# Attention and gated MLP on one core: scores from the ninth pair on as three rounded products in place of one f32 product

## The chip, the cores and the metric

The kernel runs as one program on one core of a Trainium2 chip. The metric is device time in microseconds, from the program's start to its end, the median of several runs. The profile shows one further execution, instruction by instruction.

## The reference

Eight batches of eight heads go through causal attention with decay; the eight heads of a batch are then laid side by side and go through a gated MLP with a product over the sequence.

```python
batch, n_heads, seq, head_dim = (8, 8, 576, 64)

scores = scale * np.matmul(q, k.transpose(0, 1, 3, 2))
log_f = np.log(np.clip(f, 0.0001, 1.0))
cum = np.cumsum(log_f, axis=-1)
decay = cum[:, :, :, None] - cum[:, :, None, :]
scores = np.where(causal, -1000000000.0, scores + decay)
attn = np.exp(scores - max); attn = attn / (sum + 1e-09)
x = np.matmul(attn, v)            # heads side by side: 576 x 512 per batch

h = np.maximum(x @ w_in, 0.0)     # w_in 512 x 1024
u, v = (h[..., :512], h[..., 512:])
v_n = (v - mu) / np.sqrt(var + 1e-06)
v_s = np.einsum('ts,bsd->btd', w_spatial, v_n) + b_spatial[None, :, None]
return (u * v_s) @ w_out
```

All inputs and outputs are float32.

## The kernel before

The 64 heads are worked on as 32 pairs, P = 0 to 31; four pairs make a batch. A pair's q and k lie transposed in one tile `qk_t` (128 partitions x 1216 columns, L239): head 0 on partitions 0 to 63, head 1 on 64 to 127, 640 columns of q and 576 of k. In the last 128 columns of q the 64 tail queries of each head stand in a block of their own, with zeros beside them, so that one product over all 128 partitions gives the tail of both heads.

The scores of a pair are made in three parts. `score_piece` (L316) makes the causal blocks i = 0 to 3, of 128 queries and 128 (i + 1) keys, for each head from its own 64 partitions. The *first piece* is i = 2, 1, 0 (products of 384, 256 and 128 columns for each head), the *second piece* is i = 3 (512 columns). `scores_tail` (L362) makes the *tail* in two products of 288 columns (L370, traced under the helper's line L233). Each product is one f32 matmul, which the trace shows as two matmul instructions. `in_one_piece` (L217) keeps the products of a piece together and lets the first one wait for the readers that free its PSUM banks; banks 0 and 1 also hold the attention product, and DVE's subtraction into `xl` (L513) frees them.

Behind the scores, DVE's `lowest` (L306) adds the decay tile `dk` or `dt` and takes the row minimum, ACT makes the exponentials (L337, the tail's L375), DVE the reciprocals (L352, L353), and POOL multiplies by them (`share`, L314). From P = 8 on (`moved`, L393) DVE transposes the weights in 32 x 32 blocks into `mid` (L456, the tail also L381), and SP's queue moves them by 16 transfers into `e` (L463), from where PE makes the attention product (L488, L493). Its result is split into a rounded high part `xh` (fp32r, ACT, L510) and a rest `xl` (DVE, L513). The MLP, called expert work here, uses such pairs everywhere: each of its products is three fp32r matmuls (L233), high by high, high by rest, rest by high, one matmul instruction each.

`attention` (L714) works on pair P and makes the scores of P + 1: it prepares P + 1 (`prep`, L237: transfers of `qk_t`, `dk`, `dt`), masks the decay tiles on POOL (`mask`, L275, lines L280, L282, L286, called *selects* below), sends the weights of P to `e`, makes the scores of P + 1 with their tail, and then the attention product of P. The driver at the end (L874) interleaves the units of `attention` with those of `moe` (L744) by their progress. A scheduler then fixes the order on each engine, so the order of the rows is part of what a change changes. Within each engine instructions run in order.

Buffers that the change touches: `qk_t` has two buffers under the tag "qk"; the small tiles `nm` and `sm` six each; the output tile `o` (L847) two; `load_rest` (L176) brings the remaining weights through the tags "gt0", "gt1" and "o", with 1, 1 and 2 buffers; a tile of zeros `zm` (L63), read only by warming matmuls in the first stage, lives for the whole program.

Of the kernel before, what the change touches and what calls it, by code (L numbers as in the profile page):

```python
# [23 lines left out]
TL = 512  # L24
# [14 lines left out]
def attn_gmlp_kernel(ctx: ExitStack, tc: tile.TileContext, qk, v, f, w_in, w_sp, b_sp, w_out, out):  # L39
# [21 lines left out]
    make_identity(nc, ident)  # L61

    zm = cst.tile([128, 512], BF16, name="zm")  # L63
    G.memset(zm, 0.0)

# [110 lines left out]
    def load_rest(n, w_v, dh, dl, mark=None):  # L176

        raw = mo.tile([128, 2, 128, 2], U32, name="w64", tag=("gt0", "gt1", "o")[n % 3], bufs=(1, 1, 2)[n % 3])
        w = mo.tile([128, 2, 128], U32, name="w32", tag="GH", bufs=3)
        t = mo.tile([128, 2, 128], U32, name="wa", tag="GH", bufs=3)  # L180
        r, c = slice(2 * (n % 2), 2 * (n % 2) + 2), slice(128 * (n // 2), 128 * (n // 2) + 128)
        load64(w_v[:, r, c, :], dh[:, r, c], dl[:, r, c], raw, w[:], t[:], mark)
# [54 lines left out]
    def prep(P):  # L237

        qk_t = wk.tile([128, QK], F32, name="qk_t", tag="qk", bufs=2)  # L239
        SY.dma_start(out=qk_t, in_=qk[P])  # L240
        yield
# [11 lines left out]
        for h in range(2):  # L253
            SY.dma_start(out=dt[64 * h:64 * h + 64, :], in_=row_of(P, h, 640, S, 64))
        yield

    def columns(rt):
# [51 lines left out]
    def share(P, t, r):  # L309
# [3 lines left out]
        else:  # L313
            G.tensor_scalar(out=t, in0=t, scalar1=r, scalar2=1.0, op0=ALU.mult, op1=ALU.mult)  # L314

    def score_piece(P, qk_t, piece):  # L316

# [4 lines left out]

        def product(i, h):
            ps, c, _ = at[i, h]
            p, n = slice(64 * h, 64 * h + 64), 128 * (i + 1)
            return lambda: T.matmul(ps[:, c:c + n], qk_t[p, n - 128:n], qk_t[p, 640:640 + n], start=True, stop=True)  # L326

        in_one_piece([product(i, h) for i in reversed(piece) for h in range(2)])
        return at
# [9 lines left out]
    def scores(P):  # L339

        qk_t, dk, _ = tab[P]
        tt, _ = turn(P)
        nm = [wk.tile([128, 4], F32, name="nm", tag="nm", bufs=6) for h in range(2)]
        sm = [wk.tile([128, 4], F32, name="sm", tag="sm", bufs=6) for h in range(2)]
        for piece in ((0, 1, 2), (3,)):
# [16 lines left out]
    def scores_tail(P):  # L362
        qk_t, _, dt = tab.pop(P)
        _, tl = turn(P)
        nm = wk.tile([128, 4], F32, name="nm", tag="nm", bufs=6)
        sm = wk.tile([128, 4], F32, name="sm", tag="sm", bufs=6)
        for j in range(2):
            k0 = 288 * j
            sc = bank(2 + j)
            mm(sc[:, 0:288], qk_t[:, TL:640], qk_t[:, 640 + k0:928 + k0], True, True)  # L370
            freed[2 + j] = lowest(tl[:, k0:k0 + 288], sc[:, 0:288], dt[:, k0:k0 + 288], nm[:, j:j + 1])
            yield 485
# [13 lines left out]
    def keep_warm(n):  # L386
        for _ in range(n):
            mm(warm[0], zm[:, 0:128], zm[:, 0:512], True, True)

# [136 lines left out]
    def first(ws):  # L526
# [23 lines left out]
        def period(P):  # L550
# [7 lines left out]
            sb = wk.tile([128, 2, 1], F32, name="sb", tag="sb", bufs=2)  # L558
            nt = wk.tile([128, 4], F32, name="nm", tag="nm", bufs=6)
            st = wk.tile([128, 4], F32, name="sm", tag="sm", bufs=6)  # L560

# [89 lines left out]
            late.append((X, st))  # L651

        for c in range(NJ):
            blocks[c] = load_first(ws, c)
# [11 lines left out]
        rt = next(rows)  # L666
        warm.append(bank(5, False))
        keep_warm(16)
# [75 lines left out]
    def moe(b):  # L744
# [89 lines left out]
        if b % 2 == 1:  # L834
            yield from w_out_tile(b, *[[g[:, j, :] for j in range(NJ)] for g in gt[0]],
                                  [(b - 1, TL, 0, 64), (b, TL, 64, 64)])

    def w_out_tile(b, ghi, glo, dst):
        ps = acc(b)
        n = 0  # L840
        for j in range(NJ):
# [3 lines left out]
            yield 648  # L845
        tag, bufs = ("vx", 2) if b == B - 1 and nps[0] % 3 else ("o", 2)
        o = mo.tile([128, DM], F32, name="o", tag=tag, bufs=bufs)  # L847
# [78 lines left out]
```

## Time and profile before

| what | value |
|---|---|
| median of 3 runs | 746.35 us (745.24 to 753.86) |
| the profiled execution | 752.48 us, of which the span from first to last instruction is 750.3 |
| PE, matmuls | 700.4 us busy (93%), 4709 instructions |
| DVE / POOL / ACT | 480.3 / 380.1 / 369.2 us busy |
| mean granted clock of PE | 0.979 of full speed |
| L326, the two pieces, PE | 512 instructions |
| L233 `sc<-qk_t`, the tail, PE | 128 instructions |

The profile gives for every instruction its start and duration; times are in microseconds from the start of the span. Matmuls are pipelined, so the step from one matmul's start to the next one's says what a matmul costs, not its duration. PEld is the weight load of PE, SPq the DMA queue of SP. In a waits view, "A <- B" means that A sat idle until B ended.

### The profile page before, as it was taken

The numbers are of one execution on the slowest core, as the hardware profiler recorded it, in microseconds if no ns is written. First come the engines' busy times: TensorE is split into PE (matmuls) and PEld (weight loads), VectorE is DVE, ScalarE is ACT, GpSimd is POOL, SyncE is SP. The second block draws the span as 40 slices with busy tenths as digits, with TensorE's granted clock in tenths as the row PEclk, the third lists the DMA queues.
The fourth block names the chain that finished last, engine by engine and source line by source line (L and its number), as shares of the span: only waits on it lengthen the run. The fifth ranks groups of instructions, "written<-read, shape, count | busy, mean of one in ns | idle before, by whom it ended". The sixth has DMA issues, their size and how long they took to land.

```text
span 750.3 us, 14594 instructions
## 1 busy us (share of the span) xinstructions
PE 700.4 (93%) x4709; PEld 554.1 (74%) x4709; DVE 480.3 (64%) x1597; ACT 369.2 (49%) x1028; POOL 380.1 (51%) x703
## 2 busy tenths in 40 slices
PE   7878979789989898999999999999999999999997
PEld 3545757558778586797778777788779787899886
DVE  6787787855676575667666766767666766821332
ACT  6866586663544344645444444544454435521231
POOL 3887555584554453544475454635464455611241
PEclk9999999999999899999999999999999999999999
DMA  7855344246657777557874687657965686330001
GB/s 234 240 151 144 108 145 133 78 127 184 191 160 188 194 188 206 155 147 204 213 204 136 179 220 226 178 114 203 227 172 151 176 226 178 84 88 29 29 1 70
DMA packets 52749, 117.82 MB, mean 157 GB/s; under 512 B 10305, under 2 KB 14401, under 8 KB 52674
## 3 DMA queue, kind: packets, MB, share of 16 engines
q1 hardware_dynamic: 48082, 108.64, 53.7%
q10 hardware_dynamic: 4592, 8.26, 3.2%
q8 instruction: 37, 0.61, 0.4%
q14 instruction: 38, 0.31, 0.2%
HBM read 67.78 MB, written 9.75 MB: 103 GB/s over the span
## 4 chain that ended last, share of the span: by engine, by line
PE 52%; DVE 8%; POOL 8%; ACT 6%; issue 5%; DMA 2%; SPq 2%; ACTq 0%; POOLq 0%; DVEq 0%
PE ps L233 34%; PE sc L326 6%; PE sc L488 5%; POOL tt L314 4%; PE sc L233 3%; ACT tt L337 3%; DMA e<-mid 2%; PE tp L233 2%; DVE mid L456 2%; SPq L463 1%; PE sc L493 1%; DVE tt L306 1%; POOL vnl L782 1%; DVE st L774 1%; ACT o L851 1%
## 5 line engine op out<-in xcount | busy, mean ns | idle before, releaser
L337 ACT ACTIVATE tt<-tt,nm 128x384 f32<-128x384 f32 (+2 forms) x240 | 132.7, 554 | 69.0 <-DVE nm L306 66.4
L314 POOL TENSOR_SCALAR tt<-tt,sm 128x128 f32<-128x128 f32 x208 | 110.0, 549 | 49.3 <-DVE sm L353 47.0
L456 DVE STREAM_TRANSPOSE mid<-tt 128x128 f32<-128x128 f32 x192 | 90.7, 494 | 30.7 <-POOL tt L314 26.1
L827 POOL TENSOR_TENSOR gl<-u,gh 128x256 fp32r<-128x256 f32 (+1 forms) x64 | 51.4, 805 | 100.7 <-ACT gh L826 99.6
L326 PE MATMUL sc<-qk_t 64*128 64x128 f32 (+3 forms) x512 | 90.3, 473 | 9.2 <-DVE nm L306 4.8
L233 PE MATMUL ps<-xh,winh 128*128 128x256 f32 (+1 forms) x232 | 71.8, 312 | 4.2 <-DVE vx L772 2.8
L233 PE MATMUL ps<-sph,vnh 128*128 128x256 f32 (+1 forms) x240 | 74.1, 309 | 0.7 <-ACT o L851 0.7
L326 PEld LDWEIGHTS sc<-qk_t 64*128 64x128 f32 x512 | 46.1, 194 | 38.6 <-issue 9.5
L306 DVE CUSTOM_DVE_ANT_1 tt<-sc,dk 128x256 f32<-128x256 f32 (+1 forms) x120 | 64.8, 550 | 13.5 <-PE sc L326 9.8
L233 PE MATMUL ps<-xh,winl 128*128 128x256 f32 (+1 forms) x232 | 70.2, 303 | 2.9 <-POOL winl L144 2.8
L233 PE MATMUL ps<-spl,vnh 128*128 128x256 f32 (+1 forms) x240 | 70.8, 295 | 0.0
L233 PE MATMUL ps<-sph,vnl 128*128 128x256 f32 (+1 forms) x240 | 70.5, 294 | 0.0
L488 PE MATMUL sc<-e,vraw 128*64 128x256 f32 (+1 forms) x576 | 65.6, 348 | 4.8 <-DVE nm L306 2.3
L233 PE MATMUL ps<-xl,winh 128*128 128x256 f32 (+1 forms) x232 | 69.9, 302 | 0.0
L826 ACT CAST gh<-u 128x256 fp32r<-128x256 f32 (+1 forms) x64 | 27.3, 431 | 68.2 <-DVE u L823 36.2
L233 PE MATMUL ps<-winh,xh 128*128 128x512 f32 x148 | 59.9, 405 | 0.4 <-ACT o L851 0.4
L782 POOL TENSOR_TENSOR vnl<-vx,vnh 128x512 fp32r<-128x512 f32 x32 | 41.0, 1287 | 35.7 <-ACT vnh L780 35.7
L306 DVE CUSTOM_DVE_ANT_0 tt<-sc,dk 128x128 f32<-128x128 f32 (+1 forms) x120 | 48.7, 419 | 14.9 <-PE sc L326 13.6
L233 PE MATMUL ps<-winl,xh 128*128 128x512 f32 x148 | 57.8, 390 | 0.0
L823 DVE TENSOR_TENSOR u<-ps,u 128x256 f32<-128x256 f32 (+1 forms) x60 | 26.7, 445 | 47.2 <-PE ps L233 47.2
L510 ACT CAST xh<-sc 128x256 fp32r<-128x256 f32 x64 | 24.9, 399 | 63.4 <-PE sc L488 40.3
L233 PEld LDWEIGHTS ps<-xh,winh 128*128 128x128 f32 x232 | 44.8, 194 | 10.9 <-DVE vx L772 5.4
(223 smaller groups left out, 1771.7 us busy)
## 6 DMA issues: line engine op xcount, KB each, us to landing
e<-mid SPq DMA_DIRECT2D x384, 100.0 KB, 2.2
qk_t<-in_dram SPq DMA_DIRECT2D x32, 608.0 KB, 5.9
dk<-rows_d SPq DMA_DIRECT2D x58, 320.0 KB, 5.3
vraw<-in_dram SPq DMA_DIRECT2D x32, 320.0 KB, 4.0
dt<-rows_d SPq DMA_DIRECT2D x58, 144.0 KB, 6.1
out_dram<-o ACTq DMA_DIRECT2D x28, 256.0 KB, 3.6
w<-in_dram SPq DMA_DIRECT2D x16, 256.0 KB, 3.0
w<-in_dram SPq DMA_DIRECT2D x4, 512.0 KB, 6.5
```

Source lines behind the costliest of these rows:

```text
L233: T.matmul(o, l, r, start=st, stop=sp)
L306: return V.tensor_tensor_reduce(out=out, in0=ps, in1=dec, scale=-0.125, scalar=3.0e38, op0=ALU.add, op1=ALU.min, accum_out=acc_)
L314: G.tensor_scalar(out=t, in0=t, scalar1=r, scalar2=1.0, op0=ALU.mult, op1=ALU.mult)
L326: return lambda: T.matmul(ps[:, c:c + n], qk_t[p, n - 128:n], qk_t[p, 640:640 + n], start=True, stop=True)
L337: last["exp", P, h, i] = A.activation(t, t, AF.Exp, bias=nm, scale=-1.0, accum_out=sm)
L456: V.transpose(out=part(middle(P)[:, 0, at:], [[32, n], [RUN, 4], [1, 32]]), in_=part(t, [[128, n], [32, 4], [1, 32]]))
L488: return lambda: T.matmul(out, vt[:, c, h, :], src, start=c == 0, stop=c == end)
L510: last[P, s0 // 256] = A.copy(xh[:, s0:s0 + n], ps[:, 0:n])
L782: G.tensor_tensor(out=tlo, in0=x, in1=f32(th[:]), op=ALU.subtract)
L823: V.tensor_tensor(out=g, in0=o, in1=g, op=ALU.mult)
L826: A.copy(gh[j][:, 0:nt], g)
L827: G.tensor_tensor(out=gl[j][:, 0:nt], in0=g, in1=f32(gh[j][:, 0:nt]), op=ALU.subtract)
```

## The change

From P = 8 on (`moved(P)`) q and k come into a tile `raw`; ACT casts all 1216 columns to fp32r (`high`), and the rest `low` = raw - high is subtracted by POOL (columns 0 to 639, the q half) and by DVE (576 columns, the k half). Each f32 product of the scores becomes three fp32r products that add up in PSUM: high by high, high by low, low by high. The first product of a pair's first piece waits for both subtractions. `raw` and `low` share the two buffers of `qk_t`; `high` has one buffer. Other buffers change too: `zm` moves into the pool of the first stage, `nm` and `sm` go from six buffers to three and four, the tag "o" from two to one, and outputs take turns between the tags "vx" (two buffers, also used by the normalization) and "o".

```diff
     def prep(P):
 
-        qk_t = wk.tile([128, QK], F32, name="qk_t", tag="qk", bufs=2)
-        SY.dma_start(out=qk_t, in_=qk[P])
+        if moved(P):
+            qk_t = apart(P)
+        else:
+            qk_t = wk.tile([128, QK], F32, name="qk_t", tag="qk", bufs=2)
+            SY.dma_start(out=qk_t, in_=qk[P])
         yield
...
+    apart_by = {}
+
+    def apart(P):
+
+        raw = wk.tile([128, QK], F32, name="raw", tag="qk", bufs=2)
+        low = wk.tile([128, QK], F32R, name="low", tag="qk", bufs=2)
+        high = wk.tile([128, QK], F32R, name="high", tag="high")
+        SY.dma_start(out=raw, in_=qk[P])
+        A.copy(high, raw)
+        apart_by[P] = []
+        for by, c in ((G, slice(0, 640)), (V, slice(640, QK))):
+            apart_by[P].append(by.tensor_tensor(out=low[:, c], in0=raw[:, c], in1=f32(high[:, c]), op=ALU.subtract))
+        return (high, high), (high, low), (low, high)
...
+    def terms_of(P, qk_t):
+        return qk_t if moved(P) else ((qk_t, qk_t),)
+
     def score_piece(P, qk_t, piece):
...
-        def product(i, h):
+        terms = terms_of(P, qk_t)
+
+        def product(i, h, k):
             ps, c, _ = at[i, h]
             p, n = slice(64 * h, 64 * h + 64), 128 * (i + 1)
-            return lambda: T.matmul(ps[:, c:c + n], qk_t[p, n - 128:n], qk_t[p, 640:640 + n], start=True, stop=True)
-
-        in_one_piece([product(i, h) for i in reversed(piece) for h in range(2)])
+            l, r = terms[k]
+            return lambda: T.matmul(ps[:, c:c + n], l[p, n - 128:n], r[p, 640:640 + n], start=k == 0,
+                                    stop=k == len(terms) - 1)
+
+        in_one_piece([product(i, h, k) for i in reversed(piece) for k in range(len(terms)) for h in range(2)],
+                     apart_by.get(P, ()))
         return at
...
-            mm(sc[:, 0:288], qk_t[:, TL:640], qk_t[:, 640 + k0:928 + k0], True, True)
+            terms = terms_of(P, qk_t)
+            for k, (l, r) in enumerate(terms):
+                mm(sc[:, 0:288], l[:, TL:640], r[:, 640 + k0:928 + k0], k == 0, k == len(terms) - 1)
...
-        nm = wk.tile([128, 4], F32, name="nm", tag="nm", bufs=6)
-        sm = wk.tile([128, 4], F32, name="sm", tag="sm", bufs=6)
+        nm = wk.tile([128, 4], F32, name="nm", tag="nm", bufs=3)
+        sm = wk.tile([128, 4], F32, name="sm", tag="sm", bufs=4)
...
-        raw = mo.tile([128, 2, 128, 2], U32, name="w64", tag=("gt0", "gt1", "o")[n % 3], bufs=(1, 1, 2)[n % 3])
+        raw = mo.tile([128, 2, 128, 2], U32, name="w64", tag=("gt0", "gt1", "o")[n % 3])
...
-        tag, bufs = ("vx", 2) if b == B - 1 and nps[0] % 3 else ("o", 2)
+        outs[0] += 1
+        tag, bufs = ("vx", 2) if (nps[0] % 3 if b == B - 1 else outs[0] % 2) else ("o", 1)
```

The scheduler's order moves with it. On PE, ahead of and in the first piece of P = 17, the kernel before has (`woh`, `wol` are MLP weights, `sc` the score banks, `ps` the MLP's):

```order
L233 MATMUL ps<-wol,gh 128x512
L233 MATMUL ps<-woh,gh 128x512
L233 MATMUL ps<-wol,gh 128x512
L326 MATMUL sc<-qk_t 128x384 x2
L326 MATMUL sc<-qk_t 128x256 x2
L326 MATMUL sc<-qk_t 128x128 x2
L233 MATMUL ps<-woh,gl 128x512 x2
L233 MATMUL sc<-qk_t 128x288 x2
L233 MATMUL ps<-sph,vnh 128x320
```

and the changed kernel:

```order
L230 MATMUL ps<-woh,gh 128x512
L230 MATMUL ps<-wol,gh 128x512
L346 MATMUL sc<-high 128x384 x2
L346 MATMUL sc<-low,high 128x384 x2
L346 MATMUL sc<-high,low 128x384 x2
L346 MATMUL sc<-high 128x256 x2
L346 MATMUL sc<-low,high 128x256 x2
L346 MATMUL sc<-high,low 128x256 x2
L346 MATMUL sc<-high 128x128 x2
L346 MATMUL sc<-low,high 128x128 x2
L346 MATMUL sc<-high,low 128x128 x2
L230 MATMUL ps<-woh,gl 128x512 x2
```

The piece stands at the same place, with nine rows of two in place of three (the two of a row are the two heads); the tail's two f32 products, next, become six.

On PE, around the second piece of P = 16, the kernel before has both tail products next to the second piece:

```order
L233 MATMUL ps<-sptb,vb 128x256
L233 MATMUL sc<-qk_t 128x288
L326 MATMUL sc<-qk_t 128x512 x2
L233 MATMUL sc<-qk_t 128x288
L233 MATMUL ps<-sph,vnh 128x256
L233 MATMUL ps<-spl,vnh 128x256
```

In the changed kernel the tail of P = 16 is begun there, and its last two products stand 23 expert matmuls later, directly ahead of the attention product (`e,vraw`):

```order
L230 MATMUL ps<-woh,gl 128x512
L230 MATMUL ps<-woh,gh 128x512
L230 MATMUL ps<-wol,gh 128x512
L230 MATMUL ps<-woh,gl 128x512
L230 MATMUL sc<-low,high 128x288
L230 MATMUL sc<-high,low 128x288
L512 MATMUL sc<-e,vraw 64x4x2x32 x2
L517 MATMUL sc<-e,vraw 64x64 x2
```

So the tail ends later against the second piece than before, by the expert work between.

On POOL, between the shares of P = 16 (`tt_84` and `tt_85` are heads 0 and 1 of the weights, `tl` the tail's) and the first piece of P = 17, the kernel before has:

```order
L280 AFFINE_SELECT dk<-dk 128x2x128
L282 AFFINE_SELECT dk<-dk 128x256
L314 TENSOR_SCALAR tt_85<-tt_85,sm 128x128
L314 TENSOR_SCALAR tt_85<-tt_85,sm 128x256
L314 TENSOR_SCALAR tt_85<-tt_85,sm 128x384
L314 TENSOR_SCALAR tt_85<-tt_85,sm 128x512
L314 TENSOR_SCALAR tl<-tl,sm 128x576
L280 AFFINE_SELECT dk<-dk 128x2x128
L282 AFFINE_SELECT dk<-dk 128x256
L286 AFFINE_SELECT dt<-dt 64x64 x2
L827 TENSOR_TENSOR gl<-u,gh 128x256
```

and the changed kernel, where the two heads are called `tt_82` and `tt_83`:

```order
L294 AFFINE_SELECT dk<-dk 128x2x128
L296 AFFINE_SELECT dk<-dk 128x256
L328 TENSOR_SCALAR tt_83<-tt_83,sm 128x128
L328 TENSOR_SCALAR tt_83<-tt_83,sm 128x256
L328 TENSOR_SCALAR tt_83<-tt_83,sm 128x384
L328 TENSOR_SCALAR tt_83<-tt_83,sm 128x512
L294 AFFINE_SELECT dk<-dk 128x2x128
L296 AFFINE_SELECT dk<-dk 128x256
L268 TENSOR_TENSOR low<-raw,high 128x640
L300 AFFINE_SELECT dt<-dt 64x64 x2
L328 TENSOR_SCALAR tl<-tl,sm 128x576
L853 TENSOR_TENSOR gl<-u,gh 128x256
```

The subtraction into `low` stands behind the selects of `dk` of both heads, and the share of the tail moves from ahead of the second head's selects to behind those of `dt`.

## Rows read from the trace of the kernel before

**Rows 1.** Busy time of the engines from 360 to 420 us.

```profile
core 0: us, PE busy (x) PEld busy (x) DVE busy (x) ACT busy (x) POOL busy (x), PEclk, DMA share, GB/s
360.00:420.00 60.00, 59.11 (x429) 47.45 (x428) 39.20 (x137) 29.55 (x84) 30.50 (x59) 1.00 0.68 180
```

**Rows 2.** PE's waits from 180 to 645 us: total, times, longest (us).

```profile
PE sc L326 <- DVE xl L513: 3.0, 2, 2.4
```

**Rows 3.** Chain of waits around P = 18: start, duration (us), what.

```profile
367.71 1.50 PE sc L326 x12
369.20 1.59 PE ps L233 x6
370.79 0.97 PE sc L233 x4
371.76 1.06 PE sc L326 x4
...
387.08 1.50 PE sc L326 x12
```

**Rows 4.** Chain of waits from P = 28 to P = 29.

```profile
584.31 1.06 PE sc L326 x4
...
586.06 3.70 PE ps L233 x23
...
592.65 3.21 PE ps L233 x13
...
608.90 0.58 PE sc L488 x4
```

**Rows 5.** Timeline of PE: fp32r matmuls of 320 and 256 columns, a load.

```profile
169.39 0.31 PE L233 MATMUL ps<-sph,vnh 128*128 128x320 f32 x1
169.54 0.31 PE L233 MATMUL ps<-spl,vnh 128*128 128x320 f32 x1
...
413.05 0.28 PE L233 MATMUL ps<-sph,vnl 128*128 128x256 f32 x1
413.17 0.28 PE L233 MATMUL ps<-sph,vnh 128*128 128x256 f32 x1
...
413.17 0.19 PEld L233 LDWEIGHTS ps<-spl,vnh 128*128 128x128 f32 x1
```

**Rows 6.** Groups by line and shape: casts and subtractions (busy us, mean ns).

```profile
L143 ACT CAST winh<-w 128x256 fp32r<-128x256 f32 x8 | 3.2, 403 | 2.8 <-POOL w L141 2.8
L159 ACT CAST sph<-wraw 128x576 fp32r<-128x576 f32 x4 | 2.6, 654 | 0.0
...
L144 POOL TENSOR_TENSOR winl<-w,winh 128x256 fp32r<-128x256 f32 x8 | 6.1, 763 | 4.6 <-ACT winh L143 4.6
L160 POOL TENSOR_TENSOR spl<-wraw,sph 128x576 fp32r<-128x576 f32 x4 | 5.7, 1418 | 5.4 <-ACT sph L159 5.4
```

**Rows 7.** Line 786 on DVE: duration in ns, least, median, most.

```profile
L786 DVE TENSOR_TENSOR vnh<-vx,vnh x8: 685/830/1141, 110.7 to 722.8; 64x512 fp32r<-64x512 f32 x8
```

**Rows 8.** Timeline of POOL ahead of P = 17 and P = 29.

```profile
346.40 0.41 POOL L280 TENSOR_SCALAR_AFFINE_SELECT dk<-dk 128x256 f32<-128x256 f32 x1 [1.10 <-DMA dk<-rows_d]
346.76 0.41 POOL L282 TENSOR_SCALAR_AFFINE_SELECT dk<-dk 128x256 f32<-128x256 f32 x1
...
593.18 0.75 POOL L314 TENSOR_SCALAR tl<-tl,sm 128x576 f32<-128x576 f32 x1
...
594.24 0.41 POOL L282 TENSOR_SCALAR_AFFINE_SELECT dk<-dk 128x256 f32<-128x256 f32 x1
```

**Rows 9.** Timeline of PE at the first pieces of P = 17 and P = 29.

```profile
347.33 0.92 PE L326 MATMUL sc<-qk_t 64*128 64x384 f32 x4
...
594.78 0.39 PE L233 MATMUL ps<-woh,gh 128*128 128x512 f32 x1
595.01 0.39 PE L233 MATMUL ps<-wol,gh 128*128 128x512 f32 x1
...
595.79 1.57 PE L326 MATMUL sc<-qk_t 64*128 64x384 f32 x12
```

**Rows 10.** SP's waits from 100 to 200 us: total, times, longest (us).

```profile
SPq L126 <- DVE wa L139: 27.7, 7, 7.2
```

More of the change, by code (lines that the diff above doesn't have):

```diff
@@ L61, in attn_gmlp_kernel @@
     make_identity(nc, ident)
-    zm = cst.tile([128, 512], BF16, name="zm")
-    G.memset(zm, 0.0)
     lnc = cst.tile([128, 3], F32, name="lnc")
@@ L342, in scores @@
         tt, _ = turn(P)
-        nm = [wk.tile([128, 4], F32, name="nm", tag="nm", bufs=6) for h in range(2)]
-        sm = [wk.tile([128, 4], F32, name="sm", tag="sm", bufs=6) for h in range(2)]
+        nm = [wk.tile([128, 4], F32, name="nm", tag="nm", bufs=3) for h in range(2)]
+        sm = [wk.tile([128, 4], F32, name="sm", tag="sm", bufs=4) for h in range(2)]
         for piece in ((0, 1, 2), (3,)):
@@ L387, in keep_warm @@
         for _ in range(n):
-            mm(warm[0], zm[:, 0:128], zm[:, 0:512], True, True)
+            mm(warm[0], warm[1][:, 0:128], warm[1][:, 0:512], True, True)
     nev = [0]
@@ L558, in period @@
             sb = wk.tile([128, 2, 1], F32, name="sb", tag="sb", bufs=2)
-            nt = wk.tile([128, 4], F32, name="nm", tag="nm", bufs=6)
-            st = wk.tile([128, 4], F32, name="sm", tag="sm", bufs=6)
+            nt = wk.tile([128, 4], F32, name="nm", tag="nm", bufs=3)
+            st = wk.tile([128, 4], F32, name="sm", tag="sm", bufs=4)
             def low(i, at):
@@ L651, in period @@
             late.append((X, st))
+        zm = ws.tile([128, 512], BF16, name="zm", bufs=1)
+        G.memset(zm, 0.0)
         for c in range(NJ):
@@ L666, in first @@
         rt = next(rows)
-        warm.append(bank(5, False))
+        warm.extend((bank(5, False), zm))
         keep_warm(16)
@@ L836, in moe @@
                                   [(b - 1, TL, 0, 64), (b, TL, 64, 64)])
+    outs = [0]
     def w_out_tile(b, ghi, glo, dst):
```

## The prediction

> **What bounds the kernel now.** I read the stretches first: from 360 to 420 us the matrix engine PE is busy 59.11 of 60 us, DVE 39.20, POOL 30.50, ACT 29.55 [rows 1]. So where the scores of P = 9 to 31 are made, PE's own time sets the pace. PE's waits agree: the largest between 180 and 645 us is 3.0 us in all, for DVE's `xl` [rows 2]. The chain through P = 18 shows what a pair's scores cost there: 1.50 us for the first piece (12 f32 matmul instructions, two to a product), 0.97 for the tail (4), 1.06 for the second piece (4); the next first piece starts at 387.08, 15 us after this second piece [rows 3]. Last I looked at a pair with less room ahead of it, P = 29: the second piece of P = 28 at 584.31, the tail's rest, 23 expert matmuls, the attention product, 13 expert matmuls [rows 4], and the first piece of P = 29 at 595.79 [rows 9]. P = 17, 21 and 25 are like it; I take P = 9 and 13 with them, six in all.
>
> **What an f32 product costs, and a rounded one.** A tail instruction has 288 columns on all 128 rows: 0.97 / 4 = 0.242 us. An fp32r instruction of 256 columns starts every 0.11 to 0.12 us, one of 320 every 0.15 [rows 5], one of 512 every 0.23 [rows 9]; for 288 I take 0.13. An f32 instruction is thus nearly two streams of its columns, an f32 product four; three rounded products are three. In the two pieces the heads overlap: at the tail's rate the second piece has 2 steps of 0.242 x 512 / 288 = 0.43, 0.86 us for both heads together, and 0.20 of its 1.06 is fixed (one head after the other would be 1.72). The first piece has 2 x 0.242 x (384 + 256 + 128) / 288 = 1.29 and 0.21 fixed.
>
> **Tail:** six instructions of 0.13 = 0.78 for 0.97: -0.19. **Second piece:** three steps of 0.23, and 0.20, 0.89 for 1.06: -0.17. **First piece:** 384 columns lie between 320 and 512, about 0.175, 0.525 for three; 256 columns 3 x 0.115 = 0.345. For 128 columns no rounded row exists. From below it is half of 256, 0.057; from above an f32 product's four streams, 0.215. I take 0.11, next to the 256-column row and to an f32 instruction of 128 columns (0.242 x 128 / 288 = 0.108), since each step loads weights of its own: 0.33. Sum 1.20, and 0.21 fixed, 1.41 for 1.50: -0.09. Together -0.45 us a pair; 24 pairs make -10.8 us on PE. The bounds of the 128-column step make that -14.6 (0.057) and -3.2 (0.215).
>
> The Trainium skill has a rule that speaks against this ("TensorE: Matmul & The Clock Gate", Part 3, What overlaps and what doesn't): a weight load runs beside a matmul only when it goes to other rows of the array. Here fp32r matmuls of 256 columns on the same 128 rows follow each other at 0.11 us with a load of 128 columns for each [rows 5], which leaves no time for a load after the matmul; so the trace is against it. What it would make of the time stands with the rivals.
>
> **What the rests cost.** ACT casts 1216 columns: 256 take 0.403 us, 576 take 0.654 [rows 6], 0.00078 us a column, so an estimate of 0.654 + 640 x 0.00078 = 1.16. POOL subtracts 640: 0.763 for 256 and 1.418 for 576 [rows 6], so 1.55. DVE subtracts 576: 512 between two such operands take 0.685 to 1.141, 0.83 in the middle [rows 7], so 0.93. Times 24 that is 28, 37 and 22 us; per 60 us with three pairs POOL goes from 31 to 35, ACT from 30 to 33, DVE from 39 to 42, and none becomes the bound by its sum.
>
> What counts is where they stand. The first piece waits for both subtractions, these for the cast, and the cast for the tail of the pair before, as there is one `high` buffer. In the long gaps 15 us hold 1.16 + 1.55 several times over, and POOL subtracts ahead of the shares or behind one head's: I cost it at nothing. Queued behind the cast on ACT are exponentials of the second piece or the tail, 1.16 us late; POOL's shares and DVE's transposes wait for them, and at the end the transfers into `e`, which PE wants for the attention product of P = 28 at 608.90 [rows 4], 13 us after its scores are shared: that is the cover.
>
> In the short gaps it shows. POOL now runs the four shares of head 1, two selects, then the subtraction; the tail's share (0.75) goes behind it. In P = 29 the last select starts at 594.24 and takes 0.41 [rows 8]: 594.65 - 0.75 + 1.55 = 595.45. PE began at 595.79 before, and with a second piece and tail cheaper by 0.36 it is ready at 595.43: nothing lost, and I take P = 25 to go the same way. P = 17 is worse: its selects wait 1.10 us for the transfer into `dk` and end at 347.17 [rows 8], the rest would land at 348.72, and PE is ready at 347.33 [rows 9] less 0.36, 346.97: 1.75 lost. P = 21 waited for `xl` before and loses the 0.36. That is 2.1 us for four, and in proportion 3.2 for six. DVE's own subtraction (0.93) stands among the transposes of this chain, but the tail's transpose, which took about as long, leaves its place ahead of `xl`: even. If it were not, 0.9 us for each of six, 5.6.
>
> The tail's last two products stand behind the 23 expert matmuls in these pairs. So the cast starts 3.7 us later against the second piece; the attention product (589.76 to 592.65) and 3.2 us of expert work still lie between [rows 4]: 6 us for the cast's 1.16, with POOL at the shares meanwhile.
>
> **The rest of the change.** On SP the transfer of `raw` for pair P+1 waits for the subtractions of pair P, and behind it stand the transfers into `e`; in the short gap they leave when the subtraction ends, 595.45, still 13 us ahead of 608.90. Fewer weight buffers (three in place of four): SP already waits 27.7 us in seven waits for DVE's conversion [rows 10]; the sixth load would wait for the third's conversion, done before those that the next loads wait for, so nothing; without that cover one more wait of up to 7.2. Output tiles take turns over three buffers, two of them shared with the normalization, whose next use is a unit of expert work later. `nm` and `sm` come free within a pair. The zero tile's place costs nothing.
>
> **Sum.** -10.8 + 3.2 = -7.6. The profiled execution took 752.48 us, 6.1 above the median of 746.35; 752.48 - 7.6 = 744.9, and times 746.35 / 752.48 = 0.992 that is **739 us**.
>
> **The rivals.**
> *Narrow steps are dear* (0.17): fp32r with 128 columns runs at four streams, 0.215 us. For: no row shows fp32r under 256 columns. Against: 320 and 256 columns fall in step. It adds 0.315 x 24 = 7.6: 752.5, or 746.
> *The rests are late* (0.10): all six short gaps go as P = 17, and POOL's subtraction is stretched as DVE's row is (1.141 / 0.685 = 1.67) to 2.6 us: 6 x (1.75 + 1.05) = 16.8 in place of 3.2, which leaves +6.0: 758.5, or 752. For: POOL's wait for `dk` in P = 17. Against: P = 29.
> *The heads do not overlap* (0.05), the slower side: in f32 the halves run together, of fp32r no row shows it. One after the other, first pieces gain 1.20 and second ones 0.69, +1.89 x 24 = +45 on my sum: 790, or 784. It decides once more than a sixth (7.6 / 45) fails to overlap.
> *No weight load beside the stream* (0.02): a load of 0.11 ahead of each step. First piece 9 x 0.11 + 3 x (0.175 + 0.115 + 0.057) + 0.21 = 2.24, second 0.33 + 0.69 + 0.20 = 1.22, tail 6 x 0.24 = 1.44; against 1.50, 1.06 and 0.97 that is +1.37 x 24 = +33: 785, or 779. The rule of the skill's page named above would do this.
> *The fixed parts go* (0.06): if the 0.21 and 0.20 belong to f32, and not to changing between halves and the whole array, 24 x 0.41 = 9.8 more are saved: 735.1, or 729. Against: from expert work to a tail, both on the whole array, the chain has no such extra (369.20 + 1.59 is 370.79 [rows 3]).
>
> **The numbers.** My forecast has 0.60. A difference of 2% is about what a measurement of this kernel can tell from no change, so the bounds are 731.4 and 761.3. Faster has the last rival's 0.06 and 0.04 of the forecast (a 128-column step of 0.057 and no late short gap); slower has the 0.07 of the two dear ones and 0.03 of the late rests; the other 0.80 is no change that can be told. The range goes from the last rival, 729, to the late rests, 752.
>
> **What would show it.** In the changed kernel's chain: first pieces of 18 instructions in 1.41 us, second ones of 6 in 0.89, tails in 0.78, the heads' instructions starting together, steps of 128 columns at 0.11. In PE's waits: POOL's `low` ahead of first pieces, some 3 us. ACT's cast 1.16, POOL's subtraction 1.55, DVE's 0.93. I am wrong if first pieces take over 1.6 us, if waits for `low` sum to over 10 us, or if PE's idle time grows elsewhere.

## The result and the profile after

| | median | runs |
|---|---|---|
| before | 747.43 us | 744.31 to 753.86, 20 runs |
| after | 754.22 us | 750.69 to 759.60, 20 runs |
| ratio | 1.009 | 95% interval 1.0067 to 1.0114 |

The changed kernel takes 6.8 us more, where 7.6 us less was forecast; 754.2 lies outside the range of 729 to 752. By 2% the two can't be told apart, by their interval they can. The profiled execution of after took 753.1 us, below its median, that of before 752.5 us, above its own: the two traces alone differ by less than the medians (their spans are 751.3 and 750.3 us).

The pieces came out as forecast. The chain of waits at P = 9 and, last line, at a later tail (start, duration in us, what; the pieces are on L346 now, the tail on L230):

```profile
174.18 1.37 PE sc L346 x18
175.55 4.32 PE ps L230 x28
179.87 0.89 PE sc L346 x6
180.76 0.60 PE sc L230 x3
...
561.21 0.78 PE sc L230 x6
```

First piece 1.37 us for 1.50, second 0.89 for 1.06 [rows 3]; a tail 0.78 for 0.97 (the one at 180.76 shows the three of its first half alone). The timeline of PE through that first piece (both heads in one row, x2):

```profile
174.11 0.44 PE L346 MATMUL sc<-high 64*128 64x384 f32 x2
174.39 0.34 PE L346 MATMUL sc<-low,high 64*128 64x384 f32 x2
174.56 0.34 PE L346 MATMUL sc<-high,low 64*128 64x384 f32 x2
174.74 0.29 PE L346 MATMUL sc<-high 64*128 64x256 f32 x2
174.86 0.29 PE L346 MATMUL sc<-low,high 64*128 64x256 f32 x2
174.98 0.29 PE L346 MATMUL sc<-high,low 64*128 64x256 f32 x2
175.10 0.23 PE L346 MATMUL sc<-high 64*128 64x128 f32 x2
175.15 0.28 PE L346 MATMUL sc<-low,high 64*128 64x128 f32 x2
175.27 0.28 PE L346 MATMUL sc<-high,low 64*128 64x128 f32 x2
175.48 0.42 PE L230 MATMUL ps<-sph,vnh 128*128 128x320 f32 x1
```

From start to start, 384 columns cost 0.17 to 0.28 us, 256 columns 0.12, 128 columns 0.05 and 0.12: a step for both heads together, whatever the loads between. Yet PE is less busy. Busy time by stretch, after:

```profile
core 0: us, PE busy (x) PEld busy (x) DVE busy (x) ACT busy (x) POOL busy (x), PEclk, DMA share, GB/s
180.00:645.00 465.00, 442.05 (x3336) 368.92 (x3334) 348.36 (x1090) 238.89 (x632) 276.75 (x474) 1.00 0.69 184
360.00:420.00 60.00, 57.33 (x446) 48.76 (x442) 44.69 (x137) 31.51 (x85) 34.78 (x62) 1.00 0.68 182
```

and before, over the same 465 us:

```profile
180.00:645.00 465.00, 451.07 (x3111) 358.67 (x3112) 311.11 (x1080) 219.68 (x621) 233.63 (x452) 0.99 0.69 184
```

From 360 to 420 us PE has 57.33 where it had 59.11, DVE 44.69 for 39.20, POOL 34.78 for 30.50 [rows 1]. Over the 465 us PE's idle time grew from 13.9 to 22.9 us. PE's waits after, from 150 to 650 us (total, times, longest):

```profile
PE ps L230 <- ACT u L827: 5.4, 5, 2.0
PE ps L230 <- POOL gl L853: 4.0, 4, 3.0
PE sc L346 <- DVE xl L537: 3.8, 2, 2.5
PE ps L230 <- DVE u L849: 3.6, 4, 0.9
PE ps L230 <- ACT o L880: 3.3, 5, 0.7
```

and before, over the same stretch:

```profile
PE sc L326 <- DVE xl L513: 3.8, 3, 2.4
PE ps L233 <- POOL gl L827: 2.7, 1, 2.7
...
PE ps L233 <- ACT o L851: 0.7, 4, 0.2
```

The waits for `xl` and `gl` were there; those for ACT's `u` and DVE's `u` are new on the list, and those for `o` grew. They belong to the expert work, whose instructions the change leaves as they were, though it moves the buffers of `o`. `low` is not among them: in the trace POOL's subtraction ends ahead of the first product in every pair, by 0.19 us in the tightest (P = 25) and by 8 us and more in 15 of the 24. The subtractions themselves (duration in ns: least, median, most):

```profile
L268 DVE TENSOR_TENSOR low<-raw,high x24: 709/770/2191, 147.9 to 625.5; 128x576 fp32r<-128x576 f32 x24
L268 POOL TENSOR_TENSOR low<-raw,high x24: 1531/1570/2547, 148.0 to 625.7; 128x640 fp32r<-128x640 f32 x24
```

Against [rows 6, 7] the median of POOL fits (1.57 us for 1.55) and that of DVE is shorter (0.77 for 0.93); the longest are 2.8 and 1.6 times as long.

### The profile page after: what moved, and what is told of

Same layout as the page of the kernel before. It is cut to its first block, busy times and chain, and to the rows that moved or that the text cites. A ratio compares the mean times of both kernels' runs of the same rounds, so it can differ in the third digit from the quotient of the medians.

```text
span 751.3 us, 15214 instructions
## 1 busy us (share of the span) xinstructions
PE 691.2 (92%) x4948; PEld 564.3 (75%) x4949; DVE 522.6 (70%) x1621; ACT 393.2 (52%) x1052; POOL 425.6 (57%) x727
## 4 chain that ended last, share of the span: by engine, by line
PE 27%; DVE 15%; POOL 14%; DMA 9%; issue 8%; ACT 7%; SPq 6%; POOLq 0%; DVEq 0%; ACTq 0%
PE ps L230 17%; POOL tt L328 6%; SPq L487 5%; DMA dt<-rows_d 4%; ACT tt L359 3%; PE sc L512 3%; DMA e<-mid 3%; DVE tt L320 2%; PE sc L346 2%; DVE mid L480 2%; PE sc L230 2%; DVE vx L804 2%; PE tp L230 1%; DVE low L268 1%; POOL mv L803 1%
## 5 line engine op out<-in xcount | busy, mean ns | idle before, releaser
L328 POOL TENSOR_SCALAR tt<-tt,sm 128x128 f32<-128x128 f32 x208 | 112.8, 561 | 20.8 <-DVE sm L375 19.6
L480 DVE STREAM_TRANSPOSE mid<-tt 128x128 f32<-128x128 f32 x192 | 92.5, 498 | 19.7 <-POOL tt L328 15.3
L230 PE MATMUL ps<-sph,vnh 128*128 128x256 f32 (+1 forms) x240 | 73.4, 306 | 7.0 <-DVE u L849 3.6
L230 PE MATMUL ps<-xh,winh 128*128 128x256 f32 (+1 forms) x232 | 70.9, 308 | 7.7 <-ACT u L827 6.3
L230 PE MATMUL ps<-spl,vnh 128*128 128x256 f32 (+1 forms) x240 | 71.1, 296 | 0.0
L230 PE MATMUL ps<-sph,vnl 128*128 128x256 f32 (+1 forms) x240 | 70.9, 295 | 0.0
L230 PE MATMUL ps<-xh,winl 128*128 128x256 f32 (+1 forms) x232 | 68.9, 298 | 2.1 <-POOL winl L141 2.1
L230 PE MATMUL ps<-xl,winh 128*128 128x256 f32 (+1 forms) x232 | 68.7, 296 | 0.0
L230 PE MATMUL ps<-winh,xh 128*128 128x512 f32 x148 | 60.7, 410 | 0.6 <-ACT o L880 0.4
L230 PE MATMUL ps<-winl,xh 128*128 128x512 f32 x148 | 58.6, 396 | 0.0
L230 PEld LDWEIGHTS ps<-sph,vnh 128*128 128x128 f32 x240 | 45.3, 189 | 12.0 <-DVE u L849 5.0
L230 PEld LDWEIGHTS ps<-xh,winh 128*128 128x128 f32 x232 | 43.8, 190 | 12.8 <-ACT u L827 8.7
L230 PE MATMUL ps<-woh,gl 128*128 128x512 f32 x112 | 43.1, 408 | 4.0 <-POOL gl L853 4.0
```

What stands on the lines that cost most here:

```text
L230: T.matmul(o, l, r, start=st, stop=sp)
L480: V.transpose(out=part(middle(P)[:, 0, at:], [[32, n], [RUN, 4], [1, 32]]), in_=part(t, [[128, n], [32, 4], [1, 32]]))
```

## Experiments

Each ratio is to the kernel before, timed beside it on the same chip, with its 95% interval. The scheduler sets the order anew for each kernel, but for the last three.

### Buffers, products, load, wait

**e1_buffers**: the change's buffers alone, scores in f32.

> The buffers of the change alone (zero tile moved, nm, sm, o and the weight buffers as in the change), the scores as f32 products as before; no high, no low. Theory A (the first piece waits for cast and rests): nothing of the loss is here, ratio to before 0.997 to 1.003. Theory B (the 28 + 45 + 37 us of extra work on ACT, DVE and POOL delay what frees PE's banks): the same, 0.997 to 1.003. Theory C (fewer output and weight buffers, and other addresses of the tiles, cost): 1.005 to 1.015, and the expert matmuls of 256 columns on sph at 0.119 us apart as in the changed kernel instead of 0.113.

Measured: 1.0035 (1.0002 to 1.0068). That lies between the theories' ranges. I had these edits at nothing; the median is worth 2.6 us, and it may be hardly anything.

**e2_products**: three products per score, from one high tile cast once.

```diff
+            A.copy(kept[0], raw)
...
+        return ((kept[0], kept[0]),) * 3
```

> The buffers of the change and three fp32r products for each f32 product, but nothing made for them: all pairs from 8 on multiply the one high tile cast for pair 8, so the scores of the later pairs are wrong; raw is still transferred for each pair. This leaves out 23 casts, all rests and every wait for them. PE's saving alone: by the measured pieces (1.37, 0.89, 0.78 us against 1.50, 1.06, 0.97) 0.49 x 24 = 11.8 us. Theories A and B: ratio 0.982 to 0.988. Theory C: 0.988 to 1.000.

Measured: 0.9966 (0.9940 to 0.9991). This is outside the range of theories A and B and inside that of C. The gain on PE exists, at less than the forecast's size. In the profile a wait of 6.4 us for a transfer into `e`, between the scores of P = 9 and P = 10, takes some of it; from the first piece of P = 13 to that of P = 31 the stretch is 10.6 us shorter than before's 376.7 (259.8 to 636.5 there).

**e3_load** and **e4_wait**: a cast and both subtractions per pair, read by nobody; then the same, waited for.

```diff
+        low = wk.tile([128, QK], F32R, name="low", tag="qk", bufs=2)
+        A.copy(low, raw)
...
+            i = by.tensor_tensor(out=low[:, c], in0=raw[:, c], in1=f32(low[:, c]), op=ALU.subtract)
+            apart_by[P].append(i)
```

> As e2_products, and for each pair the cast (into low) on ACT and the subtractions on POOL and DVE are made in the same sizes, but no product reads them or waits for them. Theory A: as e2_products, 0.982 to 0.990. Theory B: most of the loss is here already, 0.998 to 1.010, with PE's waits for ACT u, DVE u, POOL gl and ACT o summing to over 14 us between 150 and 650 us.

> As e3_load, and the first product of each pair from 8 on waits for both subtractions of its pair, as in the change; but the cast does not wait for the tail of the pair before, since no product reads the tile that it writes. Theory A in the form that the wait for POOL and DVE costs: 0.995 to 1.010, at least 0.006 above e3_load. Theory A in the form that the single high buffer costs (cast behind the tail): as e3_load, within 0.004. Theory B: as e3_load.

Measured: 1.0393 (1.0356 to 1.0431) and 1.0395 (1.0359 to 1.0430). The wait adds nothing to the load. But the load is not the change's: the cast now stands early in ACT's queue and blocks it until `raw` has landed, as ACT's waits show (in the changed kernel the cast waits for `raw` once, 3.3 us):

```profile
ACT low L269 <- DMA raw<-in_dram: 42.0, 15, 5.3
```

So these two say what a badly placed cast costs, and only of the wait something on the change.

### The address, the cast, and who subtracts

From here on `sm` has five buffers, so that the tiles after it begin at multiples of 64 bytes as before.

**f1_aligned**: nothing else.

```diff
-        sm = wk.tile([128, 4], F32, name="sm", tag="sm", bufs=4)
+        sm = wk.tile([128, 4], F32, name="sm", tag="sm", bufs=5)
```

> The changed kernel with five `sm` buffers for four, so that `high` and every tile allocated after it begin at multiples of 64 bytes again, as in the kernel before. Theory A (the extra cast and subtractions on ACT, POOL and DVE cost the pairs; the address costs a little beside them): the 256-column steps on `sph` fall from 0.120 to 0.113 us, some 450 of them, 2.7 us or 0.0035; ratio 1.004 to 1.007 for 1.009. Theory B (the address is most of the loss): 1.000 or lower. Theory C (the address has nothing to do with it, and the 1.0035 of the buffers alone was the order of the work): 1.008 to 1.011, steps as before.

Measured: 1.0082 (1.0048 to 1.0116). The 80 steps of 256 columns on `sph` by `vnh` between 180 and 640 us have a median of 0.118 us, with 0.119 in after, 0.121 in e1_buffers and 0.114 before. The address at 64 bytes isn't it (theory C); why these steps are slower stays open. PE, DVE, ACT and POOL run the same rows in the same order here as in the changed kernel. This kernel is the base of the next.

**f2_cast_only**: no subtraction.

```diff
-        low = wk.tile([128, QK], F32R, name="low", tag="qk", bufs=2)
...
-        return (high, high), (high, low), (low, high)
+        return ((high, high),) * 3
```

> As the aligned kernel, without the rests: the cast on ACT runs for each pair and frees its tile after the tail as in the change, but nothing is subtracted, and all three products multiply `high` by `high` (the scores are those of the rounded q and k alone). Theory A1 (the subtractions on DVE and POOL carry the loss): 0.984 to 0.992, about what products without any cast or rest gave (0.9966) less the address share (0.0035). Theory A2 (the cast on ACT, or the single `high` buffer that ties it to the tail, carries it): 1.000 to 1.006, as the aligned kernel.

Measured: 0.9978 (0.9951 to 1.0006), short of A1's range but 1.04% under f1_aligned: what made the loss left with the subtractions. Cast, `high`'s single buffer and its tie to the tail are hardly it: without them (e2_products) the ratio was much the same, though in another order.

**f3_pool_subs** and **f4_dve_subs**: all 1216 columns by POOL, by DVE.

```diff
-        for by, c in ((G, slice(0, 640)), (V, slice(640, QK))):
+        for by, c in ((G, slice(0, QK)),):
```

> As the aligned kernel, with all 1216 columns of the rest subtracted by POOL, in one instruction of some 2.9 to 3.5 us; DVE subtracts nothing. Theory A1a (what hurts is the stretch of DVE's subtraction to 2.2 us where POOL subtracts beside it, and the delay of `xl` and `u` behind it): 0.996 to 1.002. Theory A1b (POOL is the engine short of time, since shares and `gl` wait behind the subtraction): 1.010 to 1.020, with PE's waits for POOL `gl` over 8 us.

> As the aligned kernel, with all 1216 columns subtracted by DVE, in one instruction of 1.4 to 1.6 us; POOL subtracts nothing. Theory A1a (the stretch of the two subtractions beside each other hurts): 0.996 to 1.002, since no subtraction is longer than 1.6 us and POOL is as free as before. Theory A1b (POOL is short of time): also 0.996 to 1.003. Theory A1c (DVE is short of time, whatever POOL does): 1.005 to 1.015, with PE's waits for DVE `xl` and `u` up by over 5 us against the aligned kernel.

Measured: 1.0148 (1.0106 to 1.0189) and 1.0111 (1.0061 to 1.0162). Theory A1a's ranges are missed by both: with one engine subtracting, the two subtractions can't stretch each other, and it is no better. That doesn't clear the stretch in the changed kernel, since lengths and order differ here too. Neither engine takes the whole rest for nothing. The ratios lie in the ranges of A1b and A1c, but the waits that these named are not there: PE's waits for POOL's `gl` were 3.0 us in the first, not over 8, and in the second there are none for DVE's `xl` and `u`; ACT's `vx` stood out in both (6.0 and 11.2).

### Load or wait, POOL or DVE

**f5_unread**, **f8_wait_only**, **f6_unread_pool**, **f7_unread_dve**: the rests computed but read by nobody; 8 columns each, but waited for; POOL's half unread; DVE's half unread.

```diff
-            apart_by[P].append(by.tensor_tensor(out=low[:, c], in0=raw[:, c], in1=f32(high[:, c]), op=ALU.subtract))
-        return (high, high), (high, low), (low, high)
+            by.tensor_tensor(out=low[:, c], in0=raw[:, c], in1=f32(high[:, c]), op=ALU.subtract)
+        return ((high, high),) * 3
```

> As the aligned kernel, with both rests computed at the same places in the queues, but no product reads them or waits for them: all three products multiply `high` by `high`. Theory L (the time that the subtractions take from DVE and POOL makes the loss): 1.006 to 1.011, as the aligned kernel (1.008). Theory W (the wait of the first product for two engines' queues makes it, the load is covered): 0.995 to 1.001, as the kernel with the cast alone (0.998).

> As the aligned kernel, but each subtraction is of 8 columns in place of 640 and 576, at its place in POOL's and DVE's queues; the first product waits for both as in the change; all three products multiply `high` by `high`. Theory L: 0.996 to 1.002, as with the cast alone. Theory W: 1.006 to 1.011.

> As the kernel with unread rests, with POOL's half (640 columns) alone; DVE subtracts nothing, and products are of `high` alone. If POOL's load makes the loss: 1.005 to 1.010. If DVE's does: 0.996 to 1.001. If each adds its part: 1.001 to 1.005.

> As the kernel with unread rests, with DVE's half (576 columns) alone; POOL subtracts nothing, and products are of `high` alone. If DVE's load makes the loss: 1.005 to 1.010. If POOL's does: 0.996 to 1.001. If each adds its part: 1.001 to 1.005.

Measured: unread 1.0043 (1.0016 to 1.0069), between the two theories; wait only 0.9966 (0.9939 to 0.9993), within theory L's range; POOL's half 0.9900 (0.9873 to 0.9928), below every range I gave; DVE's half 1.0104 (1.0063 to 1.0146). The wait for subtractions of 8 columns costs nothing, and the traces of after and f1_aligned show none for the long ones, so theory W falls; why the unread kernel is 0.39% under f1_aligned stays open. But DVE's half alone costing more than both halves, and POOL's less than none, can't be load alone. Between these kernels the scheduler's order differs too: against f5_unread by some 40 rows on PE in f6_unread_pool and by some 1700 in f7_unread_dve.

### Relief for DVE, another split

**g1_relief** is f1_aligned, **g2_before_relief** the kernel before, with three copies taken from DVE; **g3_split** divides the rest 896 to 320.

```diff
-        (A.copy if P < 2 * PPB else V.tensor_copy)(xh[:, S:640], f32(xl[:, TL:S]))
+        A.copy(xh[:, S:640], f32(xl[:, TL:S]))
...
-                        V.tensor_copy(gt[0][r][:, j, r0:r0 + 64], f32(gg[:, 256:320]))
+                    A.copy(gt[0][0][:, j, r0:r0 + 64], f32(gh[j][:, 256:320]))
+                    G.tensor_copy(gt[0][1][:, j, r0:r0 + 64], f32(gl[j][:, 256:320]))
```

> As the aligned kernel, rests and waits included, but DVE is relieved of three copies per pair, together 1.07 us as against the 1.05 us of its subtraction: the copy of 64 columns of `xl` behind `xh` (0.468) and that of `gh` into `gt` (0.259) go to ACT, that of `gl` into `gt` (0.344) to POOL. Theory D (DVE has no room in a pair, so that what its queue gains in length is lost; POOL and ACT have it): the stretch from P=13's first piece to P=31's, which is 2.9 us longer than before in the aligned kernel and 4 to 5 us shorter where DVE subtracts nothing, becomes 3 to 6 us shorter than before; ratio 0.992 to 1.001. Theory Q (what hurts is where the subtraction stands in DVE's queue, ahead of what PE waits for, not the length of the queue): stretch 1 to 4 us longer than before, ratio 1.005 to 1.011. Theory E (ACT has no room either): stretch over 4 us longer, 1.012 and more.

> The kernel before, scores in f32, with the same three copies taken from DVE. If DVE has room in the kernel before, where PE needs 0.45 us more for a pair: 0.998 to 1.002. If DVE's queue sets the pace there too: 0.985 to 0.995, and then the relief, not its meeting with the rests, is what the first run shows.

> As the aligned kernel, with the rest divided 896 to POOL and 320 to DVE, for 640 and 576. Theory D: DVE's part falls by some 0.45 us a pair, of about 0.4 us that 1.05 us of DVE cost, so that the stretch from P=13 to P=31 is 0 us longer than before, plus or minus 2; 1.002 to 1.008. If POOL's columns cost as much as DVE's: stretch 2 to 5 us longer, 1.007 to 1.012. If every column that POOL has more costs as in the kernel where POOL has them all (stretch 7.5 us longer at 1216 for 2.9 at 640): 4 to 6 us longer, 1.010 to 1.014.

Measured: 1.0035 (1.0006 to 1.0064), the stretch 1.9 us longer (257.1 to 635.7); 0.9962 (0.9938 to 0.9986); 1.0125 (1.0094 to 1.0156), the stretch 14.3 us longer (255.1 to 646.1). The relief is worth 0.47% in the changed kernel, barely more than the noise of the two, and 0.38% in the old one, between the two ranges given: a shorter DVE queue seems to pay in both, and with it in both the change still costs 0.73%. Theory D's promise of 0.992 to 1.001 is missed, theory Q's 1.005 too. Fewer columns on DVE and more on POOL made it worse, in an order that differs from f1_aligned's by some 3000 rows on PE; here PE waits for POOL's `low` ahead of first pieces, three times, 2.3 us in all. The stretch, taken from one execution each, follows neither DVE's columns nor POOL's. g2_before_relief computes what before does and is faster than both kernels, the fastest here of those that compute the whole result.

### The same order, other lengths

**h3_both8**, **h1_dve8**, **h2_pool8**: f1_aligned's order and waits on every engine, instruction by instruction. The columns are cut once the order stands, and the products read `high` where they read `low`.

```diff
+                cut = lambda a: type(a)(ap=[list(a.ap[0]), [1, 8]], offset=a.offset, dtype=a.dtype, memref=a.memref,
+                                        memsetref=a.memsetref)
+                got[at] = i.__replace__(ins=[cut(a) for a in i.ins], outs=[cut(a) for a in i.outs])
```

> The aligned kernel with every instruction in its place on every engine and every wait as it is there; only, both subtractions work on 8 columns, and the products read `high` where they read `low` (the scores are those of the rounded q and k). Theory D (the length of the subtractions makes the loss): 0.991 to 1.000, and the stretch from P=13's first piece to P=31's 3 to 6 us shorter than before, 1 us less for each 0.13%. Theory Q (the order that the rests bring into the queues makes it, whatever they take): 1.006 to 1.011, stretch 1 to 4 us longer, as the aligned kernel (1.0082, 2.9 us).

> The same, with DVE's subtraction alone cut to 8 columns; POOL's has its 640, and the products read `high` alone. Theory D with DVE as the engine short of room: within 0.002 of the kernel where both are cut. With POOL as that engine: 1.005 to 1.011. With the two stretching one another: within 0.002 of the kernel with both cut, and equal to the next run. Theory Q: 1.006 to 1.011.

> The same, with POOL's subtraction alone cut to 8 columns; DVE's has its 576, and the products read `high` alone. Theory D with DVE short of room: 1.005 to 1.011. With POOL short of room: within 0.002 of the kernel where both are cut. With the two stretching one another: within 0.002 of the kernel with both cut. Theory Q: 1.006 to 1.011.

| columns of POOL, of DVE | ratio | interval |
|---|---|---|
| 8, 8 (h3_both8) | 0.9926 | 0.9901 to 0.9950 |
| 8, 576 (h2_pool8) | 0.9960 | 0.9935 to 0.9984 |
| 640, 8 (h1_dve8) | 1.0010 | 0.9982 to 1.0037 |
| 640, 576 (f1_aligned) | 1.0082 | 1.0048 to 1.0116 |

Theory D holds by the ratios, theory Q falls: at one order, the length of the two subtractions is worth 1.56%, some 11.6 us of 747. In this order POOL's is worth 0.84%; DVE's 0.34% and the 0.38% more that shows only with both are no larger than the noise of such differences. None of the forms of theory D, which named one engine or the stretch alone, holds: h1_dve8 fits none of them, and "within 0.002" was missed by h2_pool8 too, though by less than the noise. The clock has little part in it: PE's mean granted clock in these runs was 0.981 in f1_aligned and 0.984 in h3_both8, and within the runs of either kernel 0.01 of it goes with 4 to 5 us, so an estimate is 1 to 2 of the 11.6 us.

The stretch misled me again: in h3_both8 it is 1.4 us longer (251.0 to 629.2), as its gain came before P = 13. The busy time of f1_aligned:

```profile
180.00:645.00 465.00, 443.09 (x3328) 370.13 (x3327) 348.28 (x1090) 238.08 (x629) 276.86 (x473) 0.99 0.69 183
```

and h3_both8:

```profile
180.00:645.00 465.00, 447.76 (x3405) 377.39 (x3404) 319.39 (x1111) 243.50 (x642) 243.97 (x485) 0.99 0.68 183
```

In the same 465 us PE issues 77 more matmuls. As the order is the same, the two traces can be laid beside each other matmul by matmul: h3_both8 is 1.3 us ahead where f1_aligned stands at 150 us, with hardly a subtraction done, 2.3 at 180, 8.7 at 260 and 10.2 at 645. Two kinds of places show how it gets ahead. The first stands between the scores of P = 17 and P = 18. Timeline of f1_aligned:

```profile
353.32 2.18 DVE L268 TENSOR_TENSOR low<-raw,high 128x576 fp32r<-128x576 f32 x1
353.32 1.57 POOL L268 TENSOR_TENSOR low<-raw,high 128x640 fp32r<-128x640 f32 x1
...
353.47 0.31 PE L230 MATMUL ps<-sptb,vb 66*128 66x320 f32 x1
...
355.43 0.70 DVE L480 STREAM_TRANSPOSE mid<-tl 128x512 f32<-128x512 f32 x1
355.53 0.31 PE L230 MATMUL ps<-sptb,vb 66*128 66x320 f32 x1
...
356.22 0.47 DVE L849 TENSOR_TENSOR u<-ps,u 128x320 f32<-128x320 f32 x1
...
356.75 0.42 PE L230 MATMUL ps<-sph,vnh 128*128 128x320 f32 x1 [0.91 <-DVE u L849]
```

and of h3_both8:

```profile
345.94 0.23 DVE L268 TENSOR_TENSOR low<-raw,high 128x8 fp32r<-128x8 f32 x1
...
346.10 0.70 DVE L483 STREAM_TRANSPOSE mid<-tl 128x512 f32<-128x512 f32 x1
346.10 0.31 PE L230 MATMUL ps<-sptb,vb 66*128 66x320 f32 x1
...
346.89 0.47 DVE L852 TENSOR_TENSOR u<-ps,u 128x320 f32<-128x320 f32 x1
...
348.16 0.31 PE L230 MATMUL ps<-sptb,vb 66*128 66x320 f32 x1
348.31 0.31 PE L230 MATMUL ps<-sph,vnh 128*128 128x320 f32 x1
```

A group of expert matmuls ends with the `sptb` matmul, and DVE's `u` reads its bank. In the first kernel the group ends at 353.47; the subtraction, stretched to 2.18 us, and the tail's transpose stand ahead of `u`, which begins at 356.22, 2.75 us later. In h3_both8 it begins 0.79 us later (346.10 to 346.89). PE finishes one more group meanwhile and then wants the bank back: its step behind 355.53 takes 1.22 us in place of 0.15 (348.16 to 348.31). By the starts of PE's matmuls this stands four times in f1_aligned (at 270.59, 355.53, 522.63 and 608.77, 1.07 us lost each time) and nowhere in h3_both8: 4.3 us. The changed kernel has it four times too, each behind a subtraction of 2.18 or 2.19 us. With POOL's subtraction cut (h2_pool8) none of the four is left, though DVE's keeps its 576 columns; with DVE's cut (h1_dve8) two of them lose 0.48 us still, where DVE's 8 columns took 1.60 us beside POOL's subtraction. So this part is the price of the two subtractions meeting, and some of it is still in the row of h1_dve8 in the table.

The second kind is POOL's `gl`, which PE wants as an operand. The largest such place is ahead of P = 10, in f1_aligned:

```profile
192.60 0.39 PE L230 MATMUL ps<-wol,gh 128*128 128x512 f32 x1
193.01 0.41 POOL L294 TENSOR_SCALAR_AFFINE_SELECT dk<-dk 128x256 f32<-128x256 f32 x1 [1.09 <-DMA dk<-rows_d]
193.38 1.53 POOL L268 TENSOR_TENSOR low<-raw,high 128x640 fp32r<-128x640 f32 x1
...
195.24 0.86 POOL L853 TENSOR_TENSOR gl<-u,gh 128x320 fp32r<-128x320 f32 x1
...
196.15 1.17 PE L230 MATMUL ps<-woh,gl 128*128 128x512 f32 x2 [3.16 <-POOL gl L853]
```

and in h3_both8:

```profile
189.55 0.21 POOL L268 TENSOR_TENSOR low<-raw,high 128x8 fp32r<-128x8 f32 x1
...
190.02 0.39 PE L230 MATMUL ps<-wol,gh 128*128 128x512 f32 x1
190.09 0.86 POOL L856 TENSOR_TENSOR gl<-u,gh 128x320 fp32r<-128x320 f32 x1
...
191.00 0.73 PE L230 MATMUL ps<-woh,gl 128*128 128x512 f32 x2 [0.59 <-POOL gl L856]
```

PE's step there takes 3.55 us in f1_aligned, 2.78 in h1_dve8, 1.11 in h2_pool8 and 0.98 in h3_both8: the length of POOL's subtraction makes most of it, and the later landing of `dk` ahead of it some. PE's waits for `gl` from 180 to 645 us fall from 4.2 to 0.7 us. Against these gains PE waits longer for `xl` in h3_both8 (6.0 us for 3.8), so they don't add up to the 11.6 us place by place.

## Why the prediction was wrong

**Right: PE's work.** 1.37, 0.89 and 0.78 us for the forecast's 1.41, 0.89 and 0.78; steps of 128 columns 0.05 to 0.12 for 0.11, which ends the first rival; heads in one step and no separate load, which ends the third and fourth; the second piece of exactly 0.89 speaks against the fifth. (The fourth's load of 0.11 us stands in no row; the one in [rows 5] lasts 0.19.) Measured, a pair saves 0.49 us on PE, 11.8 for 24 pairs.

**Too dear: the wait for the rests.** The cast took 1.20 us for 1.16. The 3.2 us that I charged to the short gaps were not lost there: instead of some 3 us of PE waiting for `low`, the waits view has none. The tie of the cast to the tail cost nothing that f2_cast_only shows.

**Failed: "none becomes the bound by its sum", and POOL's 1.55 in the long gaps "I cost it at nothing".** No engine did become the bound, and this was the wrong test. At fixed order the two subtractions' length costs 1.56%, 11.6 us over 24 pairs, 0.48 us a pair: as much as the 0.49 us a pair that PE saves. I looked for who waits for the subtraction and found the first product, with room. The ones that paid stood behind it on the same queues: the expert work's `u` on DVE and `gl` on POOL, without which PE has no free bank or no operand. My test of cover named shares, transposes and the transfers into `e`, and left the expert work on these engines out. "PE's idle time grows elsewhere", the last of my signs, is what happened: 13.9 to 22.9 us.

**Also failed, smaller: durations from single rows.** For DVE I took 0.93, one figure; 0.77 in the middle and up to 2.19 where POOL subtracts at the same time was the truth, and four of the long ones stand where `u` is delayed.

**"The zero tile's place costs nothing" and the other buffers:** 0.35% (0.02 to 0.68) in e1_buffers, order or otherwise; not settled.

**The sum.** Without the rests' length, in the changed kernel's own order, 0.9926 was measured; the forecast's 739 over 746.35 is 0.990, at the edge of that interval (0.9901). The term that was missing is the 11.6 us. That the rest comes so near is in part luck: the forecast has 3.2 us for a wait that did not come, while of the 11.8 us saved on PE h3_both8 shows only 5.5; e1_buffers may hold 2.6 of what is missing there, the remainder is open. The rival "the rests are late" gave +6.0 us, near the +6.8, and POOL's subtraction did stretch to its 2.6 us (2547 ns at most); but its path, the first products of the short gaps, is contradicted by the waits, so the nearness is luck.

**Open:** how much of the 1.56% is particular to this order. At nearly the same work other orders gave other times: POOL's 640 columns alone 1.0010 in f1_aligned's order (h1_dve8) and 0.9900 in an order of their own (f6_unread_pool); DVE's 576 alone 0.9960 (h2_pool8) and 1.0104 (f7_unread_dve). So the order seems to be worth 1.1 to 1.4%, either way, and the price of the length is shown for the order of the changed kernel alone. The mean granted clock differs as well, 0.976 in f4_dve_subs and 0.979 in f7_unread_dve where before has 0.984 to 0.985; whether as cause or effect is not shown. Nor was the subtraction tried at another place of these queues.

## What to carry to other kernels

Where one engine is busy 97% of a stage, the cover of added work on another engine isn't that engine's idle share: list what stands behind the new instruction in its queue and frees a buffer or feeds an operand of the busy engine, the neighbouring stage's instructions too. An edit under a scheduler changes durations and order together; to price a duration, hold the order fixed and change only the length. Take the verdict from medians over many runs: a stretch within one trace pointed the wrong way here more than once. With the order held, lay two traces beside each other instruction by instruction: that shows where the time went.

## What was not expected of the hardware

DVE's subtraction of 576 columns takes 0.77 us, but 2.18 where POOL subtracts beside it. With DVE's cut to 8 columns (h1_dve8), POOL's longest is 1597 ns, for 2547 in after:

```profile
L268 POOL TENSOR_TENSOR low<-raw,high x24: 1537/1568/1597, 146.9 to 619.8; 128x640 fp32r<-128x640 f32 x24
```

With POOL's cut (h2_pool8), DVE's longest is 1084, for 2191:

```profile
L268 DVE TENSOR_TENSOR low<-raw,high x24: 710/772/1084, 147.4 to 620.1; 128x576 fp32r<-128x576 f32 x24
```

Both are that slow only in company, and it isn't a matter of columns: with 8 of them in h1_dve8 DVE's subtraction still took up to 1596 ns, where it began with POOL's of 1562 (at 349.06 us):

```profile
L268 DVE TENSOR_TENSOR low<-raw,high x24: 119/198/1596, 148.5 to 619.6; 128x8 fp32r<-128x8 f32 x24
```

So in such a meeting DVE's instruction ends only when POOL's has ended, or later. The Trainium skill ("GPSIMD Engine Reference", section 1, Specifications) says that GpSimd's way into SBUF is shared with VectorE and contended by DVE instructions with two SBUF inputs; these rows agree, and put its price at up to 1.4 us for one such meeting. Leaving the meeting out by giving one engine everything was still no gain (f3_pool_subs, f4_dve_subs).
